# A GpSimd multiply by a constant: the constant as the instruction's scalar in place of a constant tile

## The chip, the core and the metric

One core of a Trainium2 chip runs the whole program. The metric is the device time of one execution in microseconds (us), the median of several runs. TensorE (PE in the profile) multiplies matrices, VectorE is DVE, ScalarE is ACT, GpSimd is POOL, and SyncE (SP) issues every DMA of this kernel.

## The reference

Attention with a top-32 mask, followed by two MLPs, everything in float32:

```python
scores = scale * np.matmul(q, k.transpose(0, 1, 3, 2))          # (4, 8, 576, 576), head size 64
kth = np.partition(scores, -32, axis=-1)[..., -32:-31]
scores = np.where(scores >= kth, scores, -1e9)
attn = softmax(scores)                                          # with 1e-9 added to the sum
x = (attn @ v) as (2304, 512)
h = x @ moe_w_in;  x = (h - tanh(h)) @ moe_w_out                # 512 -> 2048 -> 512
h = x @ moe2_w_in; x = where(h > 0, h, exp(min(h, 0)) - 1) @ moe2_w_out
```

## The kernel before, in words

**Chunks and groups.** The 2304 rows are cut into six chunks of 384. A chunk's attention runs over four pairs of heads, in groups of up to three tiles of 128 queries. For each group PE makes the scores, ACT copies them to SBUF, and DVE finds the 32nd largest value of each row by four rounds of MAX8 (line 318) with three MATCH_REPLACE8 (line 332) between them. The masked exponentials `e` are made by ACT (lines 334 and 335; all three tiles of a group of chunk 0, one tile in chunk 1) or by DVE (line 339). PE transposes `e` (line 360) and multiplies it with V (line 378).

**MLPs.** Once a chunk's attention is done, its two MLPs run in steps, one for each of the 16 slices of 128 hidden units: `first` (line 460), an activation on ACT, `gate` (DVE or GpSimd), `second` (line 496). Matrices are kept as a high and a low part in float32r: `split` lets ACT round (line 126) and GpSimd subtract (line 127). The steps of one chunk run beside the attention of the next one, so DVE's top-k and PE's products alternate in time. The last chunk's steps run alone at the end.

**Weights.** The host lays a weight matrix out as 64-bit words whose lower half is one float32 weight and whose upper half another. `prepare` makes one half-slice (128 x 512 weights) of them in the first 375 us, 64 times in all:

- line 152: SP loads the raw tile (512 KB; three buffers);
- line 161 (22 of the 64 times, while PSUM banks are still free) or line 166 (the other 42): ACT multiplies the upper words by 2^-112, into PSUM or in place;
- line 162: ACT brings the lower words into a form in which DVE can combine them;
- line 164: GpSimd multiplies the upper words by `tiny`, a tile filled with 2^-60, and writes the product as float16 into the second 16 bits of each 64-bit word. The product is so small that the float16 is a zero that keeps the sign;
- line 167: DVE shifts and joins both into the weight `w`;
- lines 126 and 127: ACT and GpSimd split `w` into high and low;
- line 172: SP stores the result in DRAM, from where the chunks 1 to 5 load it.

Where line 166 scales in place, it comes after line 164, because that line still reads the unscaled words. The raw buffer comes free when line 167 is done, and then the load of three half-slices later may start.

**Order.** The code issues its operations by ticks, four to a group: loads and preparations at given ticks, MLP steps spread over them. Each engine has one queue and works it in order. What stands in that queue is not the code's order alone: the context is opened with `schedule_with_timeline_sim=True`, so a planner plays the program through with durations that it gives to each operation and puts on each engine, among the operations that are ready, the one that the code has first.

Of the kernel before, what the change touches and what calls it, by code (L numbers as in the profile page):

```python
# [93 lines left out]
def tile_topk_attention_two_mlps(  # L94
# [9 lines left out]
    nc = tc.nc  # L104
# [12 lines left out]
    tiny = const.tile([P, 512], F32, tag="tiny", name="tiny")  # L117
# [4 lines left out]
    def f(ap):  # L122
        return ap.bitcast(F32)

    def split(hi, lo, src):
        nc.scalar.activation(hi, src, copy)  # L126
        nc.gpsimd.tensor_sub(lo, src, f(hi))  # L127

    def bank(tag, name, bufs):
        return ps.tile([P, 512], F32, tag=tag, name=name, bufs=bufs)  # L130
# [10 lines left out]
    def weight_tile(half, name):  # L141
        return sb.tile([P, 2, 512], F32R, tag=f"w{half}", name=name, bufs=(WI_BUFS, WO_BUFS)[half])
# [3 lines left out]
    def prepare(m, ft, half):  # L146

        raw = sb.tile([P, 512], I64, tag="wr", name=f"wr{m}_{ft}_{half}", bufs=RAW_BUFS)
        nc.sync.dma_start(raw, (w1, w2)[m][ft][:, half * 512 : half * 512 + 512])
        words = raw.bitcast(F32).rearrange("p (n w) -> p n w", w=2)
        w = sb.tile([P, 512], F32, tag="wf", name=f"wf{m}_{ft}_{half}", bufs=2)
        low, scaled = words.bitcast(U32)[:, :, 0], words[:, :, 1]
        small = scaled
        if "wide" in stage:
            small = bank(f"acc{stage['at'] % 3}", f"sc{m}_{ft}_{half}", 1)
            stage["at"] += 1
        if small is not scaled:  # L160
            nc.scalar.activation(small, scaled, copy, scale=2.0**-112)
        nc.scalar.activation(low.bitcast(I32), low, copy, scale=2.0**-29 * (1 - 2.0**-20), bias=-0.5 + 7.5 * 2.0**-20)  # L162
        top = raw.bitcast(FP16).rearrange("p (n w) -> p n w", w=4)[:, :, 1]
        nc.gpsimd.tensor_mul(top, scaled, tiny)  # L164
        if small is scaled:
            nc.scalar.activation(scaled, scaled, copy, scale=2.0**-112)
        nc.vector.scalar_tensor_tensor(  # L167
            w.bitcast(U32), small.bitcast(U32), 3, low, op0=ALU.logical_shift_left, op1=ALU.bitwise_or
        )
        wt = weight_tile(half, f"wp{m}_{ft}_{half}")  # L170
        split(wt[:, 0], wt[:, 1], w)
        nc.sync.dma_start(f(scratch[m, ft, half]), f(wt))
        return wt

    def load_next():
        if loads:
            ci, m, ft = loads.pop(0)
            for half in range(2):
                if ci == 0 and m * NF + ft not in EARLY:
                    weights[ci, m, ft, half] = prepare(m, ft, half)  # L180
                    continue
                wt = weights[ci, m, ft, half] = weight_tile(half, f"wt{ci}_{m}_{ft}_{half}")
                nc.sync.dma_start(f(wt), f(scratch[m, ft, half]))
# [412 lines left out]
    for tick in range(FIRST_TICK, n_ticks):  # L596
        for do in before.get(tick, ()):
            do()
        while early and PREP_AT + PREP_RATE * (len(EARLY) - len(early)) <= tick:
            i = early.pop(0)  # L600
            for half in range(2):
                prepare(i // NF, i % NF, half)
# [76 lines left out]
```

## Time and profile before

| what | value |
|---|---|
| median of 3 runs | 1267.47 us (1267.06 to 1269.64) |
| the profiled execution | 1266.36 us |
| its span, first to last instruction | 1264.3 us |
| mean granted TensorE clock | 0.974 of full speed |
| PE busy | 1175.6 us (93%) |
| DVE busy | 992.0 us (78%) |
| ACT busy | 785.0 us (62%) |
| POOL busy | 603.2 us (48%) |

The span is the profiled execution without some 2 us around it. A share of busy time is an average over the whole span; the kernel has stretches with different limits, so the rows further down are cut by stretch. A matmul's end is modelled, and spans on POOL are rough.

### The profile page before, as it was taken

Reading aid. Unit: us, or ns where it says so; the run is one execution under the profiler, and the core shown is the slowest. Engines: PE = TensorE matmul, PEld = TensorE weight load, DVE = VectorE, ACT = ScalarE, POOL = GpSimd, SP = SyncE. Lnnn points to the kernel's source line nnn. Section 1 sums busy time; section 2 is a strip of 40 time slices with the busy share of each in tenths; the row PEclk is TensorE's granted clock in tenths of the full one; section 3 lists DMA queues with packets and bytes.
Section 4 is the critical chain, followed back from the end, with each engine's and each line's share of the span. In section 5 each row is a group of like instructions: output and inputs, shape, how many; then the busy total and the mean of one; then the engine's idle time right before and its main releaser. Section 6 shows DMA issues by size and latency. Waiting matters only on the chain.

```text
span 1264.3 us, 19733 instructions
## 1 busy us (share of the span) xinstructions
PE 1175.6 (93%) x6424; PEld 976.2 (77%) x6424; DVE 992.0 (78%) x1951; ACT 785.0 (62%) x1716; POOL 603.2 (48%) x629
## 2 busy tenths in 40 slices
PE   4477889989999999999999999999999999999998
PEld 2233467878779888888878888888888978889897
DVE  7999999999999999689999579898789988100111
ACT  5898868778876566465646566666555655433333
POOL 4786459779983433243433334434333422233222
PEclk9976699999999999999999999999999999999999
DMA  7886347988779665667657677756666546667672
GB/s 246 312 292 235 90 143 251 314 282 262 241 255 353 222 220 197 208 227 258 218 167 229 208 234 253 234 187 232 209 232 239 198 164 209 199 230 263 216 242 85
DMA packets 97446, 286.12 MB, mean 226 GB/s; under 512 B 12096, under 2 KB 27968, under 8 KB 97344
## 3 DMA queue, kind: packets, MB, share of 16 engines
q1 hardware_dynamic: 97344, 284.87, 67.4%
q8 instruction: 51, 0.84, 0.3%
q14 instruction: 51, 0.42, 0.1%
HBM read 246.55 MB, written 38.27 MB: 225 GB/s over the span
## 4 chain that ended last, share of the span: by engine, by line
PE 69%; DVE 14%; ACT 8%; DMA 5%; issue 3%; POOL 1%; SPq 0%; ACTq 0%; DVEq 0%; POOLq 0%
PE h L460 27%; PE acc L496 27%; PE av L378 6%; DVE vm L318 5%; DVE w L332 4%; DMA wr<-in_w_dram 4%; PE pt L360 4%; DVE wf L167 2%; PE ps L295 2%; PE ps L296 2%; DVE e L339 1%; ACT s L297 1%; ACT wr L162 1%; POOL wr L164 1%; ACT e L334 1%
## 5 line engine op out<-in xcount | busy, mean ns | idle before, releaser
L127 POOL TENSOR_TENSOR gl<-g,gh 128x384 fp32r<-128x384 f32 x192 | 206.1, 1075 | 315.0 <-ACT gh L126 292.1
L318 DVE MAX8 vm<-w 128x8 f32<-128x576 f32 x432 | 319.2, 751 | 3.9
L496 PE MATMUL acc<-wt,gh 128*128 128x512 f32 x1008 | 271.1, 398 | 0.7 <-ACT gh L126 0.7
L332 DVE MATCH_REPLACE8 w<-vm,w 128x576 f32<-128x576 f32 x288 | 213.3, 741 | 0.0
L496 PEld LDWEIGHTS acc<-wt,gh 128*128 128x128 f32 x1008 | 184.1, 188 | 33.9 <-ACT gh L126 1.6
L360 PE MATMUL pt<-ident,e 128*128 128x128 f32 (+1 forms) x720 | 119.7, 295 | 50.7 <-ACT e L335 35.8
L297 ACT ACTIVATE s<-ps 128x288 f32<-128x288 f32 (+1 forms) x320 | 124.5, 406 | 64.0 <-PE ps L296 56.5
L318 DVE MAX8 vm<-s 128x8 f32<-128x576 f32 x144 | 108.2, 752 | 62.0 <-ACT s L297 61.4
L360 PEld LDWEIGHTS pt<-ident,e 128*128 128x128 f32 (+1 forms) x720 | 90.1, 143 | 78.2 <-ACT e L335 42.0
L496 PE MATMUL acc<-wt,gl 128*128 128x512 f32 x504 | 149.9, 399 | 0.3 <-POOL gl L127 0.2
L460 PE MATMUL h<-zh,wt 128*128 128x384 f32 (+2 forms) x768 | 147.6, 325 | 2.6 <-ACT zh L515 1.8
L126 ACT ACTIVATE gh<-g 128x384 fp32r<-128x384 f32 x192 | 100.7, 526 | 74.7 <-DVE g L474 42.5
L460 PE MATMUL h<-xh,wt 128*128 128x384 f32 x672 | 144.7, 340 | 0.5 <-DVE g L479 0.2
L474 DVE SCALAR_TENSOR_TENSOR g<-t,h 128x384 f32<-128x384 f32 x96 | 52.3, 544 | 111.5 <-ACT t L466 111.3
L361 ACT ACTIVATE ph<-pt 128x384 f32<-128x384 f32 (+1 forms) x240 | 109.2, 491 | 40.9 <-PE pt L360 39.9
L460 PEld LDWEIGHTS h<-zh,wt 128*128 128x128 f32 x768 | 123.5, 188 | 13.5 <-ACT zh L515 3.2
L460 PEld LDWEIGHTS h<-xh,wt 128*128 128x128 f32 x672 | 117.7, 188 | 9.1 <-issue 1.2
L339 DVE SCALAR_TENSOR_TENSOR e<-s,vm,e 128x576 f32<-128x576 f32 x115 | 116.8, 1022 | 1.6 <-ACT e L322 0.5
L496 PEld LDWEIGHTS acc<-wt,gl 128*128 128x128 f32 x504 | 92.1, 188 | 20.2 <-issue 2.1
L164 POOL TENSOR_TENSOR wr<-wr,tiny 128x512 f16<-128x512 f32 x64 | 90.5, 1420 | 35.5 <-ACT wr L162 28.8
L332 DVE MATCH_REPLACE8 w<-vm,s 128x576 f32<-128x576 f32 x144 | 106.8, 741 | 0.0
L465 ACT ACTIVATE t<-h 128x384 f32<-128x384 f32 x96 | 46.9, 488 | 95.7 <-PE h L460 95.0
(80 smaller groups left out, 2018.2 us busy)
## 6 DMA issues: line engine op xcount, KB each, us to landing
wt<-w SPq DMA_DIRECT2D x336, 512.0 KB, 4.2
wr<-in_w_dram SPq DMA_DIRECT2D x64, 512.0 KB, 5.4
w<-wp SPq DMA_DIRECT2D x64, 512.0 KB, 4.2
kraw<-in_kT_dram SPq DMA_DIRECT2D x120, 144.0 KB, 3.9
vraw<-in_vL_dram SPq DMA_DIRECT2D x64, 160.0 KB, 3.1
qraw<-in_qT_dram SPq DMA_DIRECT2D x88, 96.0 KB, 3.3
out_dram<-o SPq DMA_DIRECT2D x16, 256.0 KB, 4.9
out_dram<-o SPq DMA_DIRECT2D x4, 128.0 KB, 4.7
```

Source lines behind the costliest of these rows:

```text
L126: nc.scalar.activation(hi, src, copy)
L127: nc.gpsimd.tensor_sub(lo, src, f(hi))
L164: nc.gpsimd.tensor_mul(top, scaled, tiny)
L297: nc.scalar.activation(s[lo:hi, cs], pt[lo:hi, :HS], copy)
L318: nc.vector.max(g.vm[:, j, min(r, 1)], u.s[t] if r == 0 else g.w[j])
L332: nc.vector.match_replace(g.w[j], v, u.s[t] if r == 0 else g.w[j], FILL)
L339: nc.vector.scalar_tensor_tensor(u.e[t], u.s[t], v[:, 7:8], u.e[t], op0=ALU.is_ge, op1=ALU.mult, accum_out=g.sum[:, j : j + 1])
L360: nc.tensor.transpose(pt[:kn, j * P : j * P + P], v.e[t][:, k0 : k0 + kn], ident)
L361: nc.scalar.activation(g.ph[:kn, blk, :nq], pt[:kn, :nq], copy)
L378: nc.tensor.matmul(pt[h * D : h * D + D, :n], v.vraw[h][:kn, blk], v.g.ph[:kn, blk, cs], start=(blk == 0), stop=(blk == NB - 1),)
L460: nc.tensor.matmul(h[:, cs], wv[:, wi, kt], xs[:, kt, cs], start=(a == 0), stop=(a == len(jobs) - 1))
L496: nc.tensor.matmul(acc[ci, m][t], gx[:, t * P : t * P + P], wt[:, wi], start=(ft == 0 and k == 0), stop=(ft == NF - 1 and k == 2),)
```

## The change

Line 164 takes its second factor from the instruction itself:

```diff
         top = raw.bitcast(FP16).rearrange("p (n w) -> p n w", w=4)[:, :, 1]
-        nc.gpsimd.tensor_mul(top, scaled, tiny)
+        nc.gpsimd.tensor_scalar_mul(top, scaled, 2.0**-60)
         if small is scaled:
             nc.scalar.activation(scaled, scaled, copy, scale=2.0**-112)
```

`scaled` (every second float32 of the raw tile, a step of 8 bytes) and `top` (one float16 in 8 bytes) are the same as before. A tensor_mul is a TENSOR_TENSOR instruction in the profile, a tensor_scalar_mul a TENSOR_SCALAR. The tile `tiny` and the instruction that fills it once (DVE, line 118) stay in the code; nothing reads the tile any more.

## Rows read from the trace of the kernel before

**Rows 1.** Busy time by stretch: us from the start, length, engines (instructions), clock, DMA.
```profile
core 0: us, PE busy (x) PEld busy (x) DVE busy (x) ACT busy (x) POOL busy (x), PEclk, DMA share, GB/s
0.00:90.00 90.00, 50.34 (x132) 27.95 (x132) 78.70 (x157) 69.58 (x145) 62.14 (x70) 0.95 0.84 284
90.00:180.00 90.00, 67.76 (x258) 40.79 (x258) 86.76 (x176) 73.75 (x167) 50.05 (x60) 0.69 0.49 159
180.00:280.00 100.00, 92.72 (x554) 78.10 (x554) 100.00 (x186) 79.20 (x166) 81.85 (x81) 1.00 0.84 278
280.00:370.00 90.00, 82.06 (x493) 68.90 (x489) 86.61 (x147) 76.54 (x167) 85.47 (x74) 1.00 0.74 239
370.00:1264.00 894.00, 882.73 (x4995) 760.44 (x4995) 639.93 (x1291) 485.95 (x1075) 323.65 (x347) 1.00 0.66 220
```

**Rows 2.** The same stretches, line 164 on POOL alone: length, busy (instructions), clock, DMA.
```profile
0.00:90.00 90.00, 30.63 (x23) 0.95 0.84 284
90.00:180.00 90.00, 13.54 (x10) 0.69 0.49 159
180.00:280.00 100.00, 21.56 (x15) 1.00 0.84 278
280.00:370.00 90.00, 24.76 (x17) 1.00 0.74 239
```

**Rows 3.** POOL's groups: line, operation, out<-in, shapes, count | busy us, mean ns | idle before.
```profile
L127 POOL TENSOR_TENSOR gl<-g,gh 128x384 fp32r<-128x384 f32 x192 | 206.1, 1075 | 315.0 <-ACT gh L126 292.1 <-PE acc L496 13.3 <-PE pt L360 6.2
L164 POOL TENSOR_TENSOR wr<-wr,tiny 128x512 f16<-128x512 f32 x64 | 90.5, 1420 | 35.5 <-ACT wr L162 28.8 <-PE ps L296 3.8 <-DMA wr<-in_w_dram 2.5
L325 POOL TENSOR_SCALAR b<-vm 128x1 f32<-128x1 f32 x8 | 1.8, 223 | 0.0
L325 POOL TENSOR_SCALAR b<-vm 128x3 f32<-128x3 f32 x7 | 1.6, 225 | 0.0
L326 POOL TENSOR_TENSOR b<-b,mb 128x3 f32<-128x3 f32 x7 | 1.4, 195 | 0.2
masks.py:199 POOL TENSOR_SCALAR_AFFINE_SELECT ident<-ident 128x128 f32<-128x128 f32 x1 | 0.3, 292 | 0.1
L667 POOL MEMSET const-float32-0.0<- 128x1 f32 x1 | 0.1, 98 | 0.2 <-issue 0.2
```

**Rows 4.** Durations ns min/median/max and first to last start, POOL, until 90 us.
```profile
L164 POOL TENSOR_TENSOR wr<-wr,tiny x23: 1336/1350/1372, 10.9 to 89.1; 128x512 f16<-128x512 f32 x23
L127 POOL TENSOR_TENSOR wp<-wf,wp x21: 1264/1276/1287, 15.6 to 87.8; 128x512 fp32r<-128x512 f32 x21
```

**Rows 5.** The same columns for line 164, from 90 us to 180 us.
```profile
L164 POOL TENSOR_TENSOR wr<-wr,tiny x10: 1342/1352/1946, 89.1 to 126.1; 128x512 f16<-128x512 f32 x10
```

**Rows 6.** The chain that ended last, its pieces on line 164: start us, us, what.
```profile
31.68 1.33 POOL wr L164
69.84 1.35 POOL wr L164
74.70 1.36 POOL wr L164
100.74 1.96 POOL wr L164
120.94 1.79 POOL wr L164
291.19 1.07 POOL wr L164
```

**Rows 7.** Who waited for line 164 in the whole span (us, times).
```profile
  ACT wr L166: 3.2, 4
  DVE wf L167: 2.4, 3
```

**Rows 8.** DVE's instructions with two inputs, by shape; line 339 of 90 to 400 us.
```profile
L167 DVE SCALAR_TENSOR_TENSOR wf<-sc,wr 128x512 uint32<-128x512 uint32 x22 | 14.9, 678 | 2.5 <-POOL wr L164 2.4
L167 DVE SCALAR_TENSOR_TENSOR wf<-wr 128x512 uint32<-128x512 uint32 x42 | 48.8, 1163 | 0.3 <-POOL qs L261 0.3
L339 DVE SCALAR_TENSOR_TENSOR e<-s,vm,e 128x576 f32<-128x576 f32 x25 | 30.7, 1231 | 0.0
```

**Rows 9.** Line 164 on POOL in the stretch 280 to 370 us, columns of rows 3.
```profile
L164 POOL TENSOR_TENSOR wr<-wr,tiny 128x512 f16<-128x512 f32 x17 | 24.8, 1474 | 0.5 <-POOL gl L127 0.2 <-ACT wr L162 0.2
```

**Rows 10.** First to last start: ACT's line 161, and POOL's line 320 until 170 us.
```profile
L161 ACT ACTIVATE sc<-wr x22: 613/634/662, 9.6 to 82.7; 128x512 f32<-128x512 f32 x22
L320 POOL TENSOR_SCALAR mb<-vm x9: 221/228/237, 16.8 to 159.2; 128x3 f32<-128x3 f32 x9
```

## The prediction

> **What bounds the kernel now.** I read the busy time by stretch first, then the rows of the changed line in the same stretches, then the chain of waits, and last the durations of POOL's and DVE's instructions by shape.
>
> From 370 us on PE is busy for 882.7 of 894 us [rows 1]: its work is fixed there and the change has no instruction in that part [rows 2]. Whatever the change does, it does before, by letting PE get its work sooner or later. Before 370 us there are three stretches with different limits. Until 180 us chunk 0's attention has no MLP beside it; DVE is the fullest engine (78.7 and 86.8 of 90 us), PE is idle for 62 us of 180, and POOL is busy 62 and 50 us of 90. From 180 to 280 us DVE is full (100.0 of 100), PE has 7.3 us idle and POOL 18. From 280 to 370 us POOL is nearly full itself, 85.5 of 90, with DVE at 86.6 and PE at 82.1 [rows 1]. There line 164 has 17 of its 64 instructions, 24.8 us, and POOL was idle only 0.5 us ahead of them [rows 2, 9]: they stand in a queue behind other work, they don't wait for their input.
>
> The chain of waits says the same on a smaller scale: line 164 has six pieces on it, five before 123 us and one at 291 us, 8.9 us together [rows 6]. Who waits for the line is little: ACT's line 166 for 3.2 us and DVE's line 167 for 2.4 us [rows 7].
>
> A second effect lies on DVE. Its line 167 takes 678 ns where one input lies in PSUM and 1163 ns where both lie in SBUF [rows 8]. The 42 of the second kind lose 42 x 0.485 = 20.4 us. Line 339, with 576 elements, would by 678 x 576/512 take 763 ns; from 90 to 400 us it takes 1231, so 25 x 0.47 = 11.7 us more are lost. In these 32 us DVE stood blocked while POOL worked.
>
> **The change, part by part.** *Removed:* 64 TENSOR_TENSOR on POOL with two f32 inputs, 1.42 us each on average, 90.5 us together [rows 3]; undisturbed it is 1.35 us [rows 4]. The two-input form without the step of 8 bytes takes 1.276 us for as many elements, so the stepped input and float16 output cost 0.074 us [rows 4]. Also gone is the read of `tiny`; filling it stays in the code and was no bound: the first line 164 starts at 10.9 us [rows 4], behind its load and ACT.
>
> *Added:* 64 TENSOR_SCALAR with one input. The trace has no such instruction on a long tile, only on one or three elements: 223 and 225 ns [rows 3]. That gives the floor and not the price of an element. The nearest row with many elements and one input is the select that builds the identity, 128 elements in 292 ns [rows 3]. If its floor is 223 ns, an element costs 0.54 ns and 512 of them 292 + 384 x 0.54 = 0.50 us: the low end. With the smallest floor that any POOL row has, 98 ns [rows 3], an element costs 1.52 ns and the sum is 0.87 us; with 0.074 for the steps and the output, 0.95 us. This is the value that I take, because it keeps most of the row's time in its elements and so doesn't lean on a favourable floor. From above no row excludes that the scalar form costs more than the one that it replaces: on the same three elements it takes 225 against 195 ns, 1.15 times [rows 3], which on 1.35 us would be 1.56 us; the far end is the longest that the instruction itself ever took, 1.95 us [rows 5]. So the difference lies between -0.85 and +0.60 us, and I take -0.40, in all 64 x 0.40 = 25.6 us of POOL's time.
>
> The GPSIMD Engine Reference of the Trainium skill, section 4.1, puts one-input elementwise work on GpSimd at roughly line rate, and section 3.1 gives 769 ns for 512 elements in its best case; no run here shows that. By that price the saving would be 0.58 us each, and as an estimate the sum below would be 7.2 us in place of 5.0.
>
> *What of it reaches the end.* Until 180 us five chain pieces become 0.40 us shorter, 2.0 us. Next in line there is DVE, which is busy 87% and 96% of those two stretches [rows 1], so half of it is swallowed: I take 1.0. Blocked DVE time: from 90 to 370 us POOL is busy 217.4 us [rows 1], 59.9 of it on line 164 [rows 2], 28%; its share of the 32 us is 8.8. With 0.95 for 1.42 us a third of that goes, 2.9 us; of it I count the part in the stretches after 180 us, where DVE is full, 2.0. From 280 to 370 us POOL is freed of 17 x 0.40 = 6.8 us; late next are DVE, with 3.4 us of idle time, and PE, with 7.9 [rows 1], and the loads of raw tiles, which wait for line 167 to free a buffer: I take 2.0. The sum is 5.0 us. The profiled execution took 1266.36 us, of which 2.1 lie around the span; so 1261.4 on its scale. The median of the runs is 1.1 higher, and the prediction is 1262.5.
>
> Line 167's loss shows what SBUF — State Buffer of the Trainium skill says in its section "Who interferes with whom": a DVE instruction with two SBUF inputs and a GpSimd instruction that reads SBUF block each other in full, whichever comes second. The trace agrees, 1163 against 678 ns [rows 8]. It speaks against more than I take: the new form reads SBUF too, so only its shorter span relieves DVE, 2.9 us. Were one input few enough to leave DVE alone, the whole 8.8 us would go, and the sum would be 5.9 higher.
>
> **The rivals.** *The scalar form is dearer.* For it: a POOL instruction's time is a loop over elements, and the only pair of rows on equal shapes has it 1.15 times slower. Against it: one read in place of two, and the select at 292 ns for 128 elements, less than a third of the 1075 ns that the two-input form takes for 384 [rows 3]. The place is 280 to 370 us, where POOL has 4.5 us to spare [rows 1] and 17 of the instructions stand: from 4.5/17 = 0.26 us dearer, that is from 1.61 us undisturbed, POOL is the bound and the stretch grows. At +0.40 it is 17 x 0.40 = 6.8, less what the idle time takes, 2.3 to 6.8; with five pieces on the early chain, 2.0, and 2.9 more of blocked DVE time, 7.2 to 11.7. I take 9: 1276.5. At the far end, +0.60, it is 5.7 to 10.2, 3.0 and 4.4, thus 13 to 18, and up to 1285.
>
> *The time is hidden.* POOL is cheaper, but before 180 us DVE's own work ends last, and after it DVE at 100% and 96% of the stretch [rows 1] sets the pace. For it: only 5.6 us of all waits are for this line [rows 7]. Against it: the blocked 32 us are DVE's own. 1266 to 1269 on the median's scale.
>
> *The order changes.* The planner gives the new operation another duration, so other operations are ready first. That it moves work far is seen in line 161, part of which the code issues in chunk 0's last two groups: its last start is 82.7 us, while the groups' line 320 runs at one in 17.8 us from 16.8 to 159.2 us [rows 10], so the eighth group is at some 141 us. What a new order gives or costs has no row; half of PE's idle time from 180 to 370 us, 15.2 us, is my measure: 7.5 us either way on top of the cases above, 1255 to 1270 with the forecast.
>
> **How the numbers follow.** A change under 0.2%, 2.5 us, can hardly be told from none here. The forecast, with its own range of 1256 to 1265, has 0.46. Hidden, or cancelled by the order: 0.20. Dearer: 0.28; slower by a worse order alone: 0.06. So faster is 0.46, the same 0.20, slower 0.34. The low end of the price alone would bring 5.0 x 0.85/0.40 = 10.6 us, 1257; with some room for the order I set 1256 below. Above I go to 1284, nearly the far end of the dearer case; some 0.05 is left out below and 0.12 above.
>
> **What would show it.** Line 164 as a TENSOR_SCALAR of 128x512 with a mean under 1.1 us confirms the price, over 1.6 us the dearer rival. If it is cheaper, line 167's mean with both inputs in SBUF should fall from 1163 towards 1120 ns or less, POOL's busy time from 280 to 370 us by some 7 us, and PE's idle time before 370 us by some 5. If it is dearer, POOL should be without a gap in that stretch and PE's idle time grow there. The reason is wrong, whatever the time, if line 164 changes by what I say and the end moves by PE waits that have nothing behind them on POOL or DVE; then the order did it.

## The result, and the profile after

The changed kernel takes 1285.9 us (median of 4 runs, 1284.2 to 1287.2) against 1268.4 us before in the same comparison: ratio 1.0141, 95% interval 1.0123 to 1.0159. It is slower by 17.5 us, where 1262.5 was forecast and the range ended at 1284. The profiled execution took 1287.2 us, its span 1285.4, 21.1 us more than before.

A correction to the description above: each 64-bit word is one float64 weight (upper half: sign, exponent and first bits of the mantissa; lower half: the rest), not two float32 weights. A half-slice is 128 x 512 of them. Line 164 makes, from the upper half, a float16 zero with the weight's sign in the upper 16 bits of the lower half. No shape or count changes by this.

The busy time by stretch of the changed kernel, columns as in [rows 1]:

```profile
0.00:90.00 90.00, 49.76 (x132) 28.52 (x132) 76.61 (x154) 65.40 (x138) 71.11 (x63) 0.95 0.73 243
90.00:180.00 90.00, 61.55 (x240) 36.83 (x238) 81.93 (x164) 71.89 (x161) 63.40 (x60) 0.67 0.57 180
180.00:280.00 100.00, 92.81 (x542) 79.61 (x541) 100.00 (x199) 80.53 (x172) 92.58 (x85) 0.98 0.80 280
280.00:370.00 90.00, 80.58 (x492) 66.33 (x491) 82.56 (x156) 72.10 (x157) 85.55 (x65) 0.94 0.62 209
```

POOL works more in three of the four stretches (71, 63 and 93 us against 62, 50 and 82 [rows 1]); in the fourth it is as busy as before, but with 65 instructions in place of 74. PE is busy for less time in the first two. The balance of PE until 400 us and after it, first of the kernel before, then of the changed one:

```profile
0.00:400.00 400.00, 322.88 (x1612) 241.85 (x1613) 381.46 (x722) 318.77 (x688) 293.41 (x297) 0.92 0.75 250
400.00:1264.00 864.00, 852.73 (x4814) 734.33 (x4812) 610.52 (x1230) 466.25 (x1030) 309.75 (x332) 1.00 0.64 215
```

```profile
0.00:400.00 400.00, 309.02 (x1534) 230.59 (x1535) 365.83 (x714) 314.39 (x681) 341.51 (x291) 0.90 0.68 230
400.00:1285.00 885.00, 873.88 (x4891) 750.99 (x4890) 612.53 (x1238) 469.68 (x1037) 317.93 (x339) 1.00 0.68 220
```

PE's idle time before 400 us goes from 77.1 to 91.0 us, +13.9; its whole busy time from 1175.6 to 1182.9, +7.3, at a lower granted clock (0.90 against 0.92 before 400 us; between 280 and 370 us 0.94 against 1.00, so part of that stretch now runs at the lower of the two levels, 1.2 GHz). The idle time after 400 us stays (11.6 and 11.5). The sum, 21.2, is the difference of the two profiled executions; the medians lie 17.5 apart. How much of the busy part belongs to the change is open: a run below with the time of the kernel before (two multiplies, old order) had PE busy for 1180.9 us in its profiled execution. All the added idle time lies before 400 us: 8.2 us before 370 us, where the prediction looked, and 5.7 between 370 and 400 us, where it took PE's work as fixed and where line 164 now still starts (up to 390.9 us).

Line 164 of the changed kernel on POOL by stretch [rows 2], then its group [rows 3], its durations with who waited for it [rows 4, 7], and its group from 280 to 370 us [rows 9]:

```profile
0.00:90.00 90.00, 43.36 (x20) 0.95 0.73 243
90.00:180.00 90.00, 28.94 (x13) 0.67 0.57 180
180.00:280.00 100.00, 30.69 (x13) 0.98 0.80 280
280.00:370.00 90.00, 35.36 (x15) 0.94 0.62 209
```

```profile
L164 POOL TENSOR_SCALAR wr<-wr 128x512 f16<-128x512 f32 x64 | 149.3, 2333 | 29.9 <-ACT wr L162 25.8
```

```profile
L164 POOL TENSOR_SCALAR wr<-wr x64: 2224/2266/2725, 10.6 to 390.9; 128x512 f16<-128x512 f32 x64
who waited for it (us, times):
  ACT wr L166: 0.9, 4
  PEld acc L496: 0.3, 1
  DVE wf L167: 0.3, 1
```

```profile
L164 POOL TENSOR_SCALAR wr<-wr 128x512 f16<-128x512 f32 x15 | 36.8, 2452 | 1.5 <-ACT wr L162 0.3
```

The new instruction takes 2333 ns on average and never under 2224, where the old one took 1420 [rows 3] and 1350 undisturbed [rows 4]: 64 x 0.913 = 58.4 us more of POOL's time. And yet hardly anybody waits for it, 1.5 us in all, less than before [rows 7]. Of the chain that ended last, line 164 has these pieces (start us, us, what), all after 200 us [rows 6]:

```profile
207.03 2.28 POOL wr L164
214.37 2.61 POOL wr L164
249.22 2.27 POOL wr L164
300.27 2.60 POOL wr L164
327.63 2.27 POOL wr L164
331.52 2.69 POOL wr L164
```

DVE's two-input instructions of the changed kernel, line 167 in the whole span and line 339 from 90 to 400 us [rows 8]:

```profile
L167 DVE SCALAR_TENSOR_TENSOR wf<-wr 128x512 uint32<-128x512 uint32 x42 | 38.3, 911 | 7.3 <-POOL b L326 3.0 <-DMA vraw<-in_vL_dram 1.4 <-POOL wp L127 1.1
L167 DVE SCALAR_TENSOR_TENSOR wf<-sc,wr 128x512 uint32<-128x512 uint32 x22 | 14.9, 677 | 0.3 <-POOL wr L164 0.3
L339 DVE SCALAR_TENSOR_TENSOR e<-s,vm,e 128x576 f32<-128x576 f32 x25 | 28.0, 1124 | 0.0
```

DVE is blocked less, not more: 1163 to 911 ns, 1231 to 1124.

A last difference is not in the diff: the planner drew other queues for the new instruction. Line 167, which joins both halves of a weight on DVE, is called a join below. In the order of the trace 56 of the 64 joins stand further back in DVE's queue than before, 3 where they were and 5 up to 5 places ahead; the last one is instruction 528 in place of 492. So two things changed, a price and an order, and the experiments had to part them.

### The profile page after: what moved, and what is told of

The parts are those of the page before. It is cut to its first block, busy times and chain, and to the rows that moved or that the text cites. A ratio compares the mean times of both kernels' runs of the same rounds, so it can differ in the third digit from the quotient of the medians.

```text
span 1285.4 us, 19775 instructions
## 1 busy us (share of the span) xinstructions
PE 1182.9 (92%) x6424; PEld 981.6 (76%) x6424; DVE 978.4 (76%) x1951; ACT 784.1 (61%) x1716; POOL 659.4 (51%) x629
## 4 chain that ended last, share of the span: by engine, by line
PE 70%; DVE 10%; ACT 8%; DMA 6%; POOL 3%; issue 3%; SPq 0%; ACTq 0%; POOLq 0%; DVEq 0%
PE h L460 28%; PE acc L496 27%; PE av L378 6%; DMA wr<-in_w_dram 5%; PE pt L360 4%; DVE vm L318 4%; DVE w L332 3%; PE ps L295 2%; PE ps L296 2%; DVE wf L167 2%; POOL wr L164 1%; ACT s L297 1%; ACT ph L361 1%; DVE e L339 1%; ACT wr L162 1%
## 5 line engine op out<-in xcount | busy, mean ns | idle before, releaser
L127 POOL TENSOR_TENSOR gl<-g,gh 128x384 fp32r<-128x384 f32 x192 | 203.4, 1061 | 324.0 <-ACT gh L126 303.6
L164 POOL TENSOR_SCALAR wr<-wr 128x512 f16<-128x512 f32 x64 | 149.3, 2333 | 29.9 <-ACT wr L162 25.8
L339 DVE SCALAR_TENSOR_TENSOR e<-s,vm,e 128x576 f32<-128x576 f32 x115 | 111.7, 978 | 1.1
```

Of the source, the lines that this page charges most:

```text
L164: nc.gpsimd.tensor_scalar_mul(top, scaled, 2.0**-60)
L339: nc.vector.scalar_tensor_tensor(u.e[t], u.s[t], v[:, 7:8], u.e[t], op0=ALU.is_ge, op1=ALU.mult, accum_out=g.sum[:, j : j + 1])
```

## The experiments

In most of them the queues of all engines are held fixed: the planner has finished, and then only the instruction of line 164 is exchanged. "Old order" means the queues of the kernel before, "new order" those of the changed kernel. The kernel before was timed beside them, 1267.7 to 1268.2 us.

### The new instruction in the old order

```diff
+    for i in (the 64 TENSOR_TENSOR that write float16, in the finished program of before):
+        replace by InstTensorScalarPtr(..., ins=[i.ins[0], 2.0**-60], op0=mult, op1=bypass)
```

> The order of every engine's queue is that of the kernel before; only line 164 is the TENSOR_SCALAR. Price theory (the instruction is 0.91 us dearer on POOL, and the new order that the planner drew adds nothing): 1282 to 1289 us, line 164 at 2.2 to 2.4 us. Order theory (most of the 17.5 us come from the new order, the old one would have hidden the price): 1267 to 1273 us with line 164 as dear.

Measured: 1305.8 us (ratio 1.0296, interval 1.0279 to 1.0313). In the old order the price alone costs 37.6 us, twice what the change cost, and above the ranges of both theories. Who made DVE wait until 420 us in this run (us, times, longest):

```profile
DVE wf L167 <- POOL wp L127: 28.2, 19, 4.6
DVE vm L318 <- ACT s L297: 13.8, 10, 5.8
DVE wf L167 <- POOL wr L164: 8.3, 8, 2.9
```

DVE's queue reaches a join before POOL has finished with the tiles, and DVE, which works in order, stands for 28.2 + 8.3 us with its top-k behind it. In the kernel before line 164 cost DVE 2.4 us [rows 7], and line 127's `wp` cost it nothing. POOL stands in PE's way as well (line 496 waited 14.2 us for line 127's `gl`).

### The old instruction in the new order

```diff
+    for i in (the 64 TENSOR_SCALAR that write float16, in the finished program of after):
+        replace by InstTensorTensor(..., ins=[i.ins[0], tiny], op=mult)
```

> The order of every engine's queue is that of the kernel after; line 164 is the TENSOR_TENSOR with the constant tile again. Price theory: 1265 to 1271 us, line 164 at 1.4 us. Order theory: 1281 to 1287 us although line 164 is back at 1.4 us.

Measured: 1290.4 us (ratio 1.0173, interval 1.0153 to 1.0194). The new order costs 22 us with the old, cheaper instruction, a little more than the order theory's range. So neither theory holds alone: price and order cost 37.6 and 22.2 us one by one, and 17.5 together.

### A cheaper line 164 in the old order: was the reach right?

Only 345 of the 512 elements are multiplied (the signs of the other 167 are left out), which gives the price that the prediction had assumed.

```diff
+        replace by InstTensorTensor(..., outs=[first 345 elements], ins=[first 345 elements of each], op=mult)
```

> The order of the kernel before; line 164 works on 345 of 512 elements, so that it takes the 0.95 us that the prediction put on the new form (the signs of the last 167 weights of each half-slice are left out). It tests the rest of the prediction's sum: if what it took for the way from POOL's time to the end is right, 1262 to 1265 us, 5 below before. If the time is hidden, 1267 to 1269. If the end follows POOL's time in proportion as it did upwards (17.5 us for 64 x 0.91 = 58 us of POOL), 64 x 0.47 = 30 us less of POOL give 9 us: 1258 to 1261.

Measured: 1262.95 us (ratio 0.9956, interval 0.9941 to 0.9971), with a mean of 1029 ns for line 164. That is 5.3 us faster; the sum of the prediction was 5.0 for 0.40 us saved each, here 0.39. The signs that it named for a cheaper line 164 came too: line 167 with both inputs in SBUF fell from 1163 to 1102 ns (it had said 1120 or less), POOL's busy time from 280 to 370 us from 85.5 to 78.7 us (some 7 less), PE's idle time before 370 us from 77.1 to 71.1 (some 5 less). So the way from price to end was right in the old order, though no run measures the three terms of its sum one by one.

The same with 8 of 512 elements (nearly all signs left out):

> The order of the kernel before; line 164 works on 8 of 512 elements, some 0.2 us (nearly all signs are left out). How much can the line give at all: by the slope of the run with 345 elements, 5.3 us for 25 us of POOL's time, 64 x 1.2 = 77 us would give 16: 1252. If PE's idle time from 180 to 370 us, 15.2 us, and the queues' order cap it: 1255 to 1261.

Measured: 1258.1 us (ratio 0.9923, interval 0.9908 to 0.9937), mean 258 ns. That lies in the capped range of the expectation, not at the 1252 of its slope: all that line 164 was worth in the old order is 10 us. Line 167 with both inputs in SBUF still takes 967 ns against some 676 for the other form: most of its blocking comes from POOL's other work, not from line 164.

### What the forms of the instruction cost by themselves

POOL's forms on 128x512, six of each, alone; at the end DVE's join 16 times, alone and beside the old and the new form. Nothing of the reference is computed.

```diff
+        g.tensor_mul(top, step, tiny)                # L44: the old line 164
+        g.tensor_scalar_mul(top, step, TINY)         # L47: the new one
+        g.tensor_scalar_mul(z, dense, TINY)          # L50: no steps, float32 out
...
+        g.tensor_scalar(z, dense, TINY, 1.0, op0=mult, op1=mult)   # L68
```

> Prices of POOL's forms by themselves on 128x512, six of each, on a short program without the rest of the work; the output is not the reference's. Also 16 of DVE's line 167 alone, beside 12 of the old form and beside 8 of the new form on POOL. Theory scalar form: TENSOR_SCALAR is dear in itself, dense f32 to f32 already at 1.9 us or more and 256 elements at about half of 512. Theory layout: dense f32 to f32 costs under 1.2 us, and the step of 8 bytes or the float16 output makes the rest. On DVE: if a one-input read on POOL blocks DVE as a two-input read does, line 167 takes some 1.2 us or more beside both forms; if not, it stays near 0.68 us beside the new form.

The groups of this kernel (line, form, count, busy us, mean ns, idle before). L53 has the stepped input alone, L59 the stepped output alone, L56 a float16 output without steps, L62 the two-input form without steps, L65 a copy, L71 the select:

```profile
L47 POOL TENSOR_SCALAR y<-x 128x512 f16<-128x512 f32 x6 | 13.3, 2214 | 1.6 <-ACT x L40 1.2
L59 POOL TENSOR_SCALAR y<-x 128x512 f16<-128x512 f32 x6 | 13.2, 2192 | 1.6 <-ACT x L40 1.2
L53 POOL TENSOR_SCALAR z<-x 128x512 f32<-128x512 f32 x6 | 9.1, 1508 | 1.6 <-ACT x L40 1.2
L56 POOL TENSOR_SCALAR z<-x 128x512 f16<-128x512 f32 x6 | 8.9, 1487 | 1.6 <-ACT x L40 1.2
L50 POOL TENSOR_SCALAR z<-x 128x512 f32<-128x512 f32 x6 | 8.9, 1487 | 1.6 <-ACT x L40 1.2
L44 POOL TENSOR_TENSOR y<-x,tiny 128x512 f16<-128x512 f32 x6 | 8.0, 1328 | 7.9 <-ACT x L40 7.5
L71 POOL TENSOR_SCALAR_AFFINE_SELECT y<-x 128x512 f16<-128x512 f32 x6 | 7.9, 1318 | 1.5 <-ACT x L40 1.2
L65 POOL CAST y<-x 128x512 f16<-128x512 f32 x6 | 7.9, 1314 | 1.5 <-ACT x L40 1.2
L62 POOL TENSOR_TENSOR z<-x,tiny 128x512 f32<-128x512 f32 x6 | 7.6, 1262 | 1.6 <-ACT x L40 1.2
L74 POOL TENSOR_SCALAR z<-x 128x256 f32<-128x256 f32 x6 | 5.1, 847 | 1.6 <-ACT x L40 1.2
L68 POOL TENSOR_SCALAR z<-x 128x512 f32<-128x512 f32 x6 | 3.7, 618 | 1.6 <-ACT x L40 1.2
```

The scalar form with one multiply is dear by itself, 1487 ns against 1262 for two inputs, (1487 - 847)/256 = 2.5 ns an element. The dense 1487 ns lie between the two theories, 1.9 us or more and under 1.2, and both parts are real: the float16 output in steps of 8 bytes adds 0.70 us. It is the steps that cost it, since float16 without steps takes 1487 ns as float32 does, and the stepped input adds 0.02. To the two-input form the stepped input and output together add 0.07. No form with that output was under 1.31 us, the select included. With a second multiply the scalar form falls to 618 ns, faster than with one.

The 16 joins alone, beside 12 of the old form, and beside 8 of the new one, and the two groups of POOL (start us, us):

```profile
118.59 11.59 DVE L79 SCALAR_TENSOR_TENSOR d<-x 128x512 uint32<-128x512 uint32 x16 [116.06 <-ACT x L40]
131.36 23.22 DVE L79 SCALAR_TENSOR_TENSOR d<-x 128x512 uint32<-128x512 uint32 x16 [1.18 <-ACT x L40]
131.41 20.49 POOL L88 TENSOR_TENSOR y<-x,tiny 128x512 f16<-128x512 f32 x12 [13.95 <-ACT x L40]
155.79 13.13 DVE L79 SCALAR_TENSOR_TENSOR d<-x 128x512 uint32<-128x512 uint32 x16 [1.21 <-ACT x L40]
155.84 19.74 POOL L93 TENSOR_SCALAR y<-x 128x512 f16<-128x512 f32 x8 [3.94 <-ACT x L40]
```

The new form blocks DVE far less. A join alone takes 692 ns. Beside the old form 12 of the 16 took some 1661 ns, one for each instruction of POOL; the other four, before and after these, took 692. Beside the new form 5 of the 16 took 1000 ns, again one for each of POOL's, and the rest 692. So an old instruction cost DVE 0.97 us and a new one 0.31. POOL lost too: 1618 ns in place of 1328, and 2400 in place of 2214 (medians).

### A scalar form at the old price

The second multiply suggested a version that does all the work: 2^-30 twice. First in the old order:

```diff
-        nc.gpsimd.tensor_mul(top, scaled, tiny)
+        nc.gpsimd.tensor_scalar(top, scaled, 2.0**-30, 2.0**-30, op0=ALU.mult, op1=ALU.mult)
```

> The order of the kernel before; line 164 is a TENSOR_SCALAR with two multiplies (2^-30 twice). Price: alone, two multiplies into dense f32 took 618 ns, and every form that writes float16 in steps of 8 bytes took at least 1314 ns, so 1.3 to 1.4 us, as dear as the old form. Blocking theory (POOL's two-input read is what blocks DVE's two-input instructions, and a one-input read does not): line 167 with both inputs in SBUF falls from 1163 ns to under 1000, and with some 10 us less of blocked DVE time the kernel takes 1258 to 1265 us. Rival (the blocked time was hidden): 1266 to 1270.

Measured: 1268.1 us (12 runs; ratio 1.0003, interval 0.9992 to 1.0014) with a mean of 1431 ns: the old price, the old time. Line 167 takes 1153 ns, so this one-input form doesn't relieve DVE, and the blocking theory's 1258 to 1265 us is out. The same line in the order that the planner draws for it:

> The same form of line 164, in the order that the planner itself draws for it. Theory fit (an order is good for the durations it was drawn for, and these are near the chip's here): within 5 us of the same form in the old order. Theory lottery (any order that is not the old one costs some 20 us, as the order of the kernel after did with the old form, 1290.4): 1280 to 1292.

Measured: 1276.7 us (ratio 1.0069, interval 1.0055 to 1.0083), mean 1418 ns. It lies between both ranges: 8.6 us over the old order, less than the lottery's 1280. And in the new order:

> The order of the kernel after, with the two multiplies in line 164. It asks why the old form was slower in that order than the new one, 1290.4 against 1285.9, though POOL works 59 us less. Blocking theory: the two-input read blocks DVE there; with a one-input read at 1.3 to 1.4 us it takes 1278 to 1285. Order theory (that order holds POOL's place in line for a slower instruction, so a cheaper one gains nothing): 1285 to 1291.

Measured: 1288.5 us (ratio 1.0167, interval 1.0152 to 1.0181), mean 1390 ns, as the order theory had it. Why the changed kernel is a little faster in this order, 1285.9, than the two cheaper forms stays open. One instruction, one price, three orders: 1268, 1277 and 1288. What the second input takes from DVE is not the matter; the order is.

### Does the new order wait for POOL at all?

```diff
+        replace by InstTensorTensor(..., outs=[first 8 elements], ins=[first 8 elements of each], op=mult)   # in the program of after
```

> The changed kernel's queues on all engines, with the old two-input operation on 8 of 512 elements in line 164's place (nearly all signs are left out; some 0.26 us each). In the old order the same cut from 1.42 us gave 10 us. Theory: the new order itself brings the raw tiles late, through DVE's line 167 standing further back, and GpSimd isn't what it waits for; then the time stays at 1280 to 1290. Rival: in the new order GpSimd is on the path too and line 164's 1.4 to 2.3 us hold it up; then at least 15 us go and it is at 1275 or less.

Measured: 1285.9 us (ratio 1.0142, interval 1.0127 to 1.0157), the time of the changed kernel, although line 164 takes a ninth of its time. The rival is out: in the new order line 164 is hidden at any price from 0.26 to 2.33 us. What SP's loads and stores of the weights waited for, and when the stores (line 172) and loads (line 152) started, of the kernel before:

```profile
SPq L152 <- DVE wf L167: 66.2, 37, 4.3
SPq L172 <- POOL wp L127: 64.2, 30, 4.4
L172 SPq DMA_DIRECT2D w<-wp x64: 319/327/536, 16.9 to 375.7; - x64
L152 SPq DMA_DIRECT2D wr<-in_w_dram x64: 327/333/543, 4.4 to 357.9; - x64
```

Of this run:

```profile
SPq L152 <- DVE wf L167: 141.0, 45, 7.7
SPq L172 <- POOL wp L127: 21.7, 14, 4.7
L172 SPq DMA_DIRECT2D w<-wp x64: 319/382/1777, 19.8 to 406.3; - x64
L152 SPq DMA_DIRECT2D wr<-in_w_dram x64: 327/331/897, 4.4 to 379.5; - x64
```

The loads wait for line 167 to free a raw buffer, 141 us in place of 66, and the last weights are stored 30 us later, with POOL nearly free of line 164. The joins stand behind other work in DVE's queue. By the timeline the lateness comes twice: the 28th join starts at 135.0 us in place of 111.3, the 32nd and the 48th only 2 to 4 us late (188.8 and 297.3 in place of 186.5 and 293.8), and the last at 401.1 in place of 372.4. So the early delay is made up and the late one stays; the last 13 joins stand 15 to 36 places further back. Of the changed kernel:

```profile
SPq L152 <- DVE wf L167: 84.6, 40, 5.1
SPq L172 <- POOL wp L127: 61.9, 30, 6.2
L172 SPq DMA_DIRECT2D w<-wp x64: 319/327/728, 19.1 to 411.2; - x64
```

SP works loads and stores in one queue, so their waits trade places: these two kinds together are 130 us before, 163 in this run and 147 in the changed kernel. A reading that no run shows by itself: in the changed kernel part of the same delay is spent in line 164 before the join's turn comes. Its last store starts 5 us later than in this run, and the time is the same.

### The order redrawn with nothing changed

```diff
+from concourse.hw_specs import TRN2Spec; TRN2Spec.GPSIMD_TENSOR_SCALAR_OP_CYCLES = (1.0, 2, 0.5)
```

> The kernel before with its old operation; only the planner is told 1 cycle an element in place of 3 for GpSimd's scalar multiply, which the kernel before has only on 1 or 3 elements, so a few ns each. That redraws the queues (2211 lines of difference on PE) and changes no instruction. Theory: a redraw alone moves the end by more than 5 us, to 1273 or more, since the old order was the better of those seen so far (1268 against 1277 to 1290). Rival: a redraw that follows the same durations is as good as the old one, 1265 to 1271; then the new order was bad because of the dearer operation that it was drawn for.

Measured: 1273.8 us (ratio 1.0047, interval 1.003 to 1.0063). The instructions are those of the kernel before; a planner price that concerns only instructions of one or three elements moved the end by 6 us, and the rival's 1265 to 1271 is out. Then two more orders for the new instruction, the same line with line 164 changed, and with (1.2, 2, 0.4):

> The new operation (2.3 us), with the planner told 1 cycle an element in place of 3 for it: a third order. Theory: with this price on GpSimd the order gives anything between the two seen, 1286 and 1306, as the planner thinks GpSimd freer than it is. Rival: the price alone sets the end in each order drawn for the new instruction stream, 1284 to 1288.

> As the run before, with 1.2 cycles: a fourth order for the new operation. Theory: 1286 to 1306, and over 3 us from the run before. Rival: 1284 to 1288 as the changed kernel, and as the run before.

Measured: 1305.8 (ratio 1.03, interval 1.0282 to 1.0319) and 1305.4 us (1.0296, 1.0278 to 1.0313). Both lie in the range of the theory, at its far end; that they would differ by over 3 us was wrong. All runs of the whole kernel together, with the place of the last join in DVE's queue, the mean of line 164 and the start of the last store:

```
order                  last join   line 164 us   last store   time us
old, 8 elements           492         0.26          368.1      1258.1
old, 345 elements         492         1.03          374.4      1263.0
before                    492         1.42          375.7      1268.4
old, two multiplies       492         1.43          378.9      1268.1
old, new instruction      492         2.32          416.5      1305.8
redrawn, old instr.       489         1.43          381.8      1273.8
own, two multiplies       485         1.42          380.5      1276.7
redrawn, new (1.0)        492         2.35          413.1      1305.8
redrawn, new (1.2)        492         2.35          415.6      1305.4
new, 8 elements           528         0.26          406.3      1285.9
new, two multiplies       528         1.39          411.6      1288.5
new, old instruction      528         1.40          412.8      1290.4
after                     528         2.33          411.2      1285.9
```

With the joins early (485 to 492) the price counts: 1268 to 1277 at 1.4 us, 1305 to 1306 at 2.3, in each of three orders. With the joins late (528) it doesn't: 1286 to 1290 at any price from 0.26 to 2.33. Which of the queues that were redrawn costs the 22 us isn't parted: there is one order of the late kind, and no run moves DVE's joins alone. The loads' waits for line 167 and the joins' late starts point to DVE. No version that does all the work beat the kernel before.

## Why the prediction was wrong

**The step that failed: the price.** "With 0.074 for the steps and the output, 0.95 us. This is the value that I take". It is 2.33, and beyond the far end too, 1.95. The nearest row, a select of 128 elements at 292 ns, stood for another operation: at 512 elements with line 164's steps the select takes 1318 ns, as dear as the old line. Two terms were mis-sized: an element of the scalar form costs 2.5 ns, not 0.54 to 1.52, and the steps and output cost 0.70 us, not the 0.074 read from the two-input form. The one pair on equal shapes, 225 against 195 ns [rows 3], pointed the right way (1.15; dense forms measured 1487/1262 = 1.18) and was set aside for the select. For one-input work the prediction cited the GPSIMD Engine Reference of the Trainium skill, roughly line rate (section 4.1) and 769 ns for 512 elements in the best case (section 3.1). This doesn't hold for the scalar form with one multiply: 1487 ns without steps.

**What was right.** The added idle time lies before 400 us, most of it before the 370 us named. The reach of the forecast, 5.0 us for 0.40 saved, measured 5.3 for 0.39. Of the signs named for the dearer rival the mean over 1.6 us came; the other came only in part (next paragraph).

**The rival that came true, and its size.** The dearer rival gave up to 1285 at 0.60 us dearer, and 1285.9 came at 0.91, but that is a coincidence. By its own formula 0.91 gives 17 x 0.91 = 15.5, less up to 4.5 of idle time, with 5 x 0.91 = 4.6 and 6.7 of blocked time: 22 to 27 us. In the old order, for which it was worked out, 37.6 were measured. It left out that DVE, working in order, would stand 36.5 us for POOL at its joins. Its place was not the right one either: from 280 to 370 us POOL should have been without a gap, and was busy for 85.6 us of 90 in the changed kernel, as before, and for 81.1 in the old order with the new form; PE's idle time there grew by 1.5 and 5.4 us. It also counted more blocked DVE time where there is less: line 167 fell by 0.09 us (1163 to 1070) in the old order with the new form.

**The order.** It had 7.5 us either way and 0.06 as a cause of its own. Measured: 6 us from a redraw with no instruction changed, 8.6 for the two multiplies, 22 for the new order with the old instruction; and in the changed kernel it took back 37.6 - 17.5 = 20 us of the price. The measure, half of PE's idle time from 180 to 370 us, had no ground: an order can lengthen idle time as well as use it. The last sign named, "PE waits that have nothing behind them on POOL or DVE", was tied to the price coming as said, and so couldn't show that here both moved.

**The read blocks.** The prediction cited SBUF — State Buffer of the Trainium skill, "Who interferes with whom", for a full block, with line 167's 1163 ns as agreement. Measured beside POOL back to back, a join took 1661 ns with the old form and 1000 with the new one, 692 alone: the block depends on POOL's form, and for the scalar form with one multiply it is far from full, 0.31 us for an instruction of 2.2. For the old form it is not full either: a join and an old instruction take 0.69 + 1.33 = 2.02 us one after the other, and 20.49 us for 12 pairs is 1.71 each. The measurement decides.

## What to carry to other kernels

Price an instruction from a row of its own operation, output type and step, not from another one-input operation; where none exists, take the nearest pair on equal shapes and leave the upper end open. Where a planner lays out the queues, an edit is a price and a redraw: run the new instruction in the old queues and the old one in the new queues before telling a cause, since here they cost 37.6 and 22.2 us alone and 17.5 together.

## What the runs showed of the hardware

GpSimd's scalar multiply of 128x512 float32 took 1487 ns with one multiply and 618 with two; with a float16 output in steps of 8 bytes 2214 with one and, in the kernel, 1342 to 1352 (medians in three orders) with two. Every form with that output took 1.31 us or more, a plain copy too. The output's steps cost the scalar form 0.70 us, its float16 type nothing. Each of GpSimd's scalar instructions with one multiply made one DVE join of two SBUF inputs 0.31 us longer, each two-input one 0.97 us.
